# Spreading a weight split over the last projections, on a kernel of infini-attention and a Fourier layer

## The chip, the core and the metric

The kernel runs on one core of a Trainium2 chip. The metric is the device time of one execution in microseconds (us), lower is better. The core has TensorE for matrix products, VectorE and ScalarE for elementwise work, GpSimd for elementwise work in on-chip memory, and SyncE, which here only issues DMAs. In the profile they are called PE, DVE, ACT, POOL and SP. Every engine works through its own instructions strictly in the order of the program and waits where an operand is not there yet.

## What is computed

Two branches work on 2048 tokens of width 576, and their outputs stand side by side.

```python
# branch A: 32 heads of width 18, 4 segments of 512 tokens, a memory M, z carried from segment to segment
for s in range(4):
    logits = q[s] @ k[s].T * scale + mask          # mask: -1e9 where query index < key index
    a_dot  = softmax(logits) @ v[s]
    a_mem  = (phi(q[s]) @ M) / (phi(q[s]) @ z + 1e-6)
    out[s] = g * a_mem + (1 - g) * a_dot
    M, z   = M + phi(k[s]).T @ v[s], z + sum(phi(k[s]))
A = concat(out) @ wo
# branch B: Fourier mixing, real part of a transform along features and then along tokens
a, b = x @ dft_hid_re.T, x @ dft_hid_im.T
B = dft_seq_re @ a - dft_seq_im @ b
```

All of it is wanted at about fp32 accuracy, so the kernel splits each operand into a rounded part and the rest ("hi" and "lo") and multiplies three times, or writes it as three bf16 parts.

## The kernel before, in words

The order of every engine's instructions is written out by hand. The program has a first phase (lines 147 to 552) that runs over the four segments `s`, and a second phase that interleaves the attention of branch A with the Fourier products of branch B on TensorE until the end.

In the first phase each segment has nine projections of queries and keys (`project_qk`, 14 matmuls each; `m` is the tile: 0 to 3 are queries, 4 to 7 keys, 8 holds what is left of both) and then four rounds `j` of the value projection (`project_v`). A round has two halves `h` of 14 matmuls and, from the second segment on, the two parts of the lookup in the memory (`lookup`), which stand after the halves on TensorE. I number a round's four TensorE steps: half 0, look part 1, half 1, look part 2. In the last segment (`s == 3`) the projections come in the order m = 0, 1, 2, 3, 8, 4, 5, 6, 7, so that `n`, the place in that order, is 4 for m = 8 and 5 to 8 for m = 4 to 7.

All these products are written to one ring of five PSUM buffers with the tag `acc`. A product can start only when the product five places earlier has been read out. After tile 8 the ring goes on as m = 4, 5, 6, 7, then round 0: half 0 (in the buffer of m = 8), look part 1 (of m = 4), half 1 (of m = 5), look part 2 (of m = 6), then round 1: half 0 (of m = 7), look part 1 (of round 0's half 0), and so on.

A projected key tile of the last segment is read out as three bf16 parts: `p0` by ScalarE (L272), the rest `r` by VectorE (L273), and then, in the nested function `rest`, `p1` from `r` (L282 on GpSimd or L284 on ScalarE) and `p2` by GpSimd (L285). `rest` is called one `tick()` later, just after `project_qk` has returned. The last reader of the PSUM buffer is `r`. A half of the value projection is read by ScalarE (L321) and VectorE (`vr`, L324); VectorE's instructions of a lookup end with `w` (L412), which is the last reader of look part 2.

The first phase also prepares the second one. `h_load` fetches the five row blocks `k` of the Fourier weights along the features, `h_split(0, k)` splits a block with `split_wk`: ScalarE rounds it (L130, twice for k = 4) and VectorE subtracts (L124; for k = 4 L126 and L127). `c_cut(n, dve)` splits input chunk `n` of the Fourier branch: ScalarE rounds two pieces (L448, L450), and one tick later VectorE subtracts twice (L453, L455). The change calls the Fourier weights "memory weights".

In the second phase the first TensorE work is one score product (L735) and `hidden(0, 0)`, which multiplies chunk 0 with the split weights in two halves (L619 to L624). The second of these halves is written to a PSUM bank that the first phase's last look part 2 had, so it starts when the last `w` is done.

Of the kernel before, what the change touches and what calls it, by code (L numbers as in the profile page):

```python
# [40 lines left out]
def infini_attention_and_fnet(ctx: ExitStack, tc: tile.TileContext, xT, wqk, w8, wv, wo, beta, xtT, cT, hT, out):  # L41
    nc = tc.nc
    act, dve, pool, pe = nc.scalar, nc.vector, nc.gpsimd, nc.tensor
# [38 lines left out]
    def chain(o, terms):  # L82
        for n, (a, b) in enumerate(terms):
            pe.matmul(o, a, b, start=n == 0, stop=n == len(terms) - 1)  # L84
# [3 lines left out]
    def later(n, fn, *a):  # L88
        due.setdefault(clock[0] + n, []).append((fn, a))

    def tick():
        clock[0] += 1
        for fn, a in due.pop(clock[0], ()):
            fn(*a)
# [26 lines left out]
    def split_wk(w, k, raw, wait=0):  # L121
        def low():
            if k < 4:
                dve.tensor_tensor(w[1][k], raw, w[0][k].bitcast(F32), OP.subtract)  # L124
            else:
                dve.tensor_tensor(w[2][:64], raw[:64], w[2][:64].bitcast(F32), OP.subtract)  # L126
                dve.tensor_tensor(w[3][64:], raw[64:], w[3][64:].bitcast(F32), OP.subtract)  # L127

        for t in (w[0][k],) if k < 4 else (w[2], w[3]):
            act.activation(t, raw, AF.Copy)  # L130
        if wait:
            later(wait, low)
        else:
            low()
# [6 lines left out]
    def weight(mk):  # L141
        return [[mk() for _ in range(4)] for _ in range(2)] + [mk() for _ in range(2)]

    def wide_tile(cols):
        return lambda: wide.tile([P, cols], F32R, name="wide", tag="wide")
# [68 lines left out]
    def phi(e, sources, hi, lo):  # L214
        for to, src in sources:
            act.activation(to, src, AF.Relu, scale=-1.0)
        act.activation(e, e, AF.Exp, scale=-1.0)
        for to, src in sources:
            dve.scalar_tensor_tensor(to, src, 0.0, to, op0=OP.max, op1=OP.add)
        dve.tensor_copy(hi, e)  # L220
        pool.tensor_tensor(lo, e, hi.bitcast(F32), OP.subtract)

    def qk_terms(s, m):
        xh, xl, xt = X[s]
        W, c = (WQ, m) if m < 4 else (WK, m - 4) if m < 8 else (W8, 0)
        cs = slice(c * P, (c + 1) * P)
        terms = []
        for k in range(4):
            terms += [(W[0][k][:, cs], xh[k]), (W[0][k][:, cs], xl[k]), (W[1][k][:, cs], xh[k])]
        return terms + [(W[2][:, cs], xt), (W[3][:, cs], xt)]  # L230
# [3 lines left out]
    def warm_up():  # L234
        o = ps.tile([P, L], F32, name="warm", tag="acc", bufs=5)
        for _ in range(38):
            pe.matmul(o[:, :P], ones, ones, start=True, stop=True)

    def open_qk(s):
        for m in range(4):  # L240
            FIRST[m] = ps.tile([P, L], F32, name="qk", tag="acc", bufs=5)
        terms = [qk_terms(s, m) for m in range(4)]
        edges = (0, 6, 14) if s else (0, 1, 2, 3, 6, 9, 14)
        for a, b in zip(edges, edges[1:]):
            for m in range(4):
                for n in range(a, b):
                    pe.matmul(FIRST[m], *terms[m][n], start=n == 0, stop=n == 13)  # L247
                if s and m == 0 and a:
                    accumulate(3, (1,))
            if s and a == 0:  # L250
                accumulate(3, (0,))
# [8 lines left out]
    def project_qk(s, m):  # L260
        if m in FIRST:
            o = FIRST.pop(m)
        else:
            o = ps.tile([P, L], F32, name="qk", tag="acc", bufs=5)
            chain(o, qk_terms(s, m))
        if m >= 4 and s < 3:
            KF[m] = sk.tile([P, L], F32, name="kf", bufs=5)
            act.activation(KF[m], o, AF.Copy)
        p = sb.tile([P, 3, L], BF16, name="p", tag="p", bufs=5)
        r = sb.tile([P, L], F32, name="r", tag="r", bufs=3)  # L270
        p0, p1, p2 = (p[:, 2 - i] if 4 <= m < 8 else p[:, i] for i in range(3))
        act.activation(p0, o, AF.Copy)  # L272
        dve.tensor_tensor(r, o, p0, OP.subtract)  # L273
        if s and (m < 4 or m == 8):
            n = P if m < 4 else 64
            c = m if m < 4 else 4
            e = sb.tile([P, L], F32, name="qe", bufs=2)[:n]
            phi(e, ((e, o[:n]),), pq_hi[:n, c], pq_lo[:, c] if m < 4 else pq_hi[64:, c])

        def rest():  # L280
            if m in (5, 6, 7):
                pool.tensor_copy(p1, r)  # L282
            else:
                act.activation(p1, r, AF.Copy)  # L284
            pool.tensor_tensor(p2, r, p1, OP.subtract)  # L285
            if m < 8:
                later(1, dma, (qd if m < 4 else kd)[s][(m % 4) * P:(m % 4 + 1) * P, :3], p)
            else:
                later(1, dma, qd[s][4 * P:, :3], p[:64])
                for i in range(3):  # L290
                    later(1, dma, kd[s][4 * P:, 2 - i], p[64:, i])

        later(1, rest)

    def k_natural(j):
# [124 lines left out]
    def h_load(ri, k):  # L420
        HRAW[ri, k] = sb.tile([P, D], F32, name="raw", tag="raw", bufs=5 if ri == 0 else 3)
        dma(HRAW[ri, k], hT[ri, k])

    def h_split(ri, k):
        if k == 0:
            HW[ri] = weight(wide_tile(D))
        split_wk(HW[ri], k, HRAW.pop((ri, k)), 2 * ri)
# [13 lines left out]
    def c_cut(n, engine=pool):  # L441
        if n < len(CHUNKS):
            raw = c_raw.pop(n)
            hi = sr.tile([P, 4, P], F32R, name="chi", bufs=3)
            lo = sr.tile([P, 4, P], F32R, name="clo", bufs=3)
            t = sr.tile([P, P], F32R, name="xtail", bufs=3) if CHUNKS[n][2] == 5 else None
            c_split[n] = hi, lo, t
            act.activation(hi, raw[:, :4], AF.Copy)  # L448
            if t is not None:
                act.activation(t, raw[:, 4], AF.Copy)  # L450

            def low():
                engine.tensor_tensor(lo, raw[:, :4], hi.bitcast(F32), OP.subtract)  # L453
                if t is not None:
                    engine.tensor_tensor(t[64:], raw[64:, 4], t[64:].bitcast(F32), OP.subtract)  # L455
            later(1, low)
# [40 lines left out]
    for s in range(NSEG):  # L497
        more = s < 3
        if s == 0:
            warm_up()  # L500
        open_qk(s)
        if s:
            memory()
        else:
            tick()
        for n, m in enumerate((0, 1, 2, 3, 8, 4, 5, 6, 7) if s else range(9)):
            project_qk(s, m)
            tick()
            if not more and n in (5, 7):
                h_split(0, (n - 5) // 2)  # L510
            if s and n < (8 if more else 4):
                copy_parts(s - 1, 2 * n)
                copy_parts(s - 1, 2 * n + 1)
            if s in (1, 2) and n >= 4:
                load_x(s + 1, n - 4)
            if not more and n == 0:
                for k in range(5):
                    h_load(0, k)
            if not more and n == 4:
                p1k.close()  # L520
                sr = ctx.enter_context(tc.tile_pool(name="sb2r", bufs=1, side="right", reuse_waits="tile"))
                attention_tiles()
            if not more and n == 4:
                c_load(0)
                c_load(1)
                stacks(sr, 0)
                stack_load(0)
            if not more and n == 6:
                c_load(2)
        for j in range(4):  # L530
            project_v(s, j, lookup(s, j) if s else iter(()))
            tick()
            for k in ((0, 1), (2, 3), (4,), ())[j] if s == 0 else ():
                load_x(1, k)
            if more and j in (1, 2):
                split_x(s + 1, j - 1)
            if not more and j == 1:
                stacks(sr, 1)
            if not more and j == 2:
                attention_constants()  # L540
            if not more and j == 0:
                h_split(0, 2)
                h_split(0, 3)
            if not more and j == 1:
                h_split(0, 4)
                c_cut(0, dve)
                c_cut(1, dve)
            if not more and j in (1, 3):
                c_load(3 + j // 2)
            if more and j:  # L550
                accumulate(j - 1)
# [512 lines left out]
```

## Time and profile before

| what | value |
| --- | --- |
| time, median of 3 runs | 1001.66 us (1001.62 to 1001.66) |
| the profiled execution: its time, its span | 1000.29 us, 998.5 us |
| TensorE clock granted | 1.000 |
| PE busy | 988.2 us, 99% |
| DVE busy | 754.1 us, 76% |
| ACT busy | 710.6 us, 71% |
| POOL busy | 635.8 us, 64% |
| last segment's projections, value rounds, first Fourier product | from about 178 us to 228 us of the span |

The busy shares are averages over the whole span. A row of the timeline has the start and the length of an instruction in us, its engine, line and operation, the tiles written and read, their shape, and in brackets how long the engine had been idle before and what released it. A count such as x2 puts neighbouring equal instructions together.

### The profile page before, as it was taken

Reading aid. Unit: us, or ns where it says so; the run is one execution under the profiler, and the core shown is the slowest. Engines: PE = TensorE matmul, PEld = TensorE weight load, DVE = VectorE, ACT = ScalarE, POOL = GpSimd, SP = SyncE. Lnnn points to the kernel's source line nnn. Section 1 sums busy time; section 2 is a strip of 40 time slices with the busy share of each in tenths; the row PEclk is TensorE's granted clock in tenths of the full one; section 3 lists DMA queues with packets and bytes.
Section 4 is the critical chain, followed back from the end, with each engine's and each line's share of the span. In section 5 each row is a group of like instructions: output and inputs, shape, how many; then the busy total and the mean of one; then the engine's idle time right before and its main releaser. Section 6 shows DMA issues by size and latency. Waiting matters only on the chain.

```text
span 998.5 us, 25584 instructions
## 1 busy us (share of the span) xinstructions
PE 988.2 (99%) x9294; PEld 923.3 (92%) x9294; DVE 754.1 (76%) x2049; ACT 710.6 (71%) x1677; POOL 635.8 (64%) x700
## 2 busy tenths in 40 slices
PE   9999999989999999999999999999999999999998
PEld 7989989889999999999999999999999999999998
DVE  6657668594678777878898888898888899998321
ACT  6667576653887877878788788877767777777243
POOL 2657576676767667666866777776767767767000
PEclk9999999999999999999999999999999999999999
DMA  7447456767578899899999997779998999988555
GB/s 253 170 126 245 187 177 239 239 231 227 147 178 212 217 236 231 201 243 221 249 231 232 211 221 198 180 200 226 222 234 215 239 238 243 244 187 188 139 153 137
DMA packets 305182, 208.92 MB, mean 209 GB/s; under 512 B 206240, under 2 KB 259872, under 8 KB 305056
## 3 DMA queue, kind: packets, MB, share of 16 engines
q1 hardware_dynamic: 304816, 207.15, 79.7%
q8 instruction: 73, 1.20, 0.5%
q14 instruction: 53, 0.43, 0.1%
q10 hardware_dynamic: 240, 0.14, 0.1%
HBM read 121.32 MB, written 57.93 MB: 180 GB/s over the span
## 4 chain that ended last, share of the span: by engine, by line
PE 89%; DVE 5%; ACT 3%; issue 1%; DMA 1%; POOL 1%; SPq 0%; DVEq 0%; ACTq 0%; POOLq 0%
PE d L574 39%; PE s L735 7%; PE d L84 6%; PE pv L853 4%; PE v L84 4%; PE qk L247 4%; PE d L619 3%; PE d L620 3%; PE d L621 3%; PE qk L84 3%; PE pv L854 2%; PE m L360 1%; PE t L809 1%; PE t L812 1%; DVE plo L836 1%
## 5 line engine op out<-in xcount | busy, mean ns | idle before, releaser
L741 DVE CUSTOM_DVE_ANT_0 s<-s,causal 128x128 f32<-128x128 f32 (+3 forms) x512 | 249.9, 498 | 101.5 <-PE s L735 92.4
L453 POOL TENSOR_TENSOR clo<-craw,chi 128x512 fp32r<-128x512 f32 x158 | 216.4, 1370 | 96.7 <-ACT chi L448 65.3
L574 PE MATMUL d<-wide,chi 128*128 128x288 f32 x1408 | 266.2, 306 | 0.4 <-DVE y L644 0.4
L574 PEld LDWEIGHTS d<-wide,chi 128*128 128x128 f32 x1408 | 211.8, 189 | 2.4 <-DVE y L644 0.6
L574 PE MATMUL d<-wide,clo 128*128 128x288 f32 x704 | 177.5, 319 | 0.0
L775 POOL TENSOR_TENSOR hl<-pf,hl 128x768 f16<-128x768 f32 x64 | 112.9, 1763 | 70.0 <-ACT hl L771 54.2
L821 ACT ACTIVATE phi<-t 128x384 f16<-128x384 f32 x128 | 61.7, 482 | 103.6 <-PE t L818 103.5
L735 PE MATMUL s<-ks,qs 108*128 108x128 bf16 (+3 forms) x512 | 133.7, 304 | 0.5 <-DVE negm L741 0.4
L764 ACT ACTIVATE pf<-s,nb 128x128 f32<-128x128 f32 (+3 forms) x256 | 128.1, 526 | 6.2
L836 DVE TENSOR_TENSOR plo<-pf,phi 128x384 f16<-128x384 f32 (+1 forms) x128 | 126.2, 986 | 0.0
L574 PE MATMUL d<-ab,chi 128*128 128x288 f32 x640 | 126.0, 306 | 0.0
L574 PEld LDWEIGHTS d<-wide,clo 128*128 128x128 f32 x704 | 118.6, 189 | 1.6
L822 ACT ACTIVATE pf<-t 128x384 f32<-128x384 f32 (+1 forms) x192 | 99.6, 519 | 6.2 <-PE t L809 6.0
L448 ACT ACTIVATE chi<-craw 128x512 fp32r<-128x512 f32 x160 | 100.2, 627 | 2.3 <-PE d L574 1.2
L574 PEld LDWEIGHTS d<-ab,chi 128*128 128x128 f32 x640 | 98.5, 189 | 0.6
L771 ACT ACTIVATE hl<-pf 128x768 f16<-128x768 f32 (+1 forms) x128 | 87.4, 730 | 2.0
L619 PE MATMUL d<-wide,chi 128*128 128x288 f32 x256 | 84.1, 329 | 2.8 <-ACT xtail L450 2.8
L574 PE MATMUL d<-ab,clo 128*128 128x288 f32 x320 | 84.8, 314 | 0.0
L620 PE MATMUL d<-wide,chi 128*128 128x288 f32 x256 | 75.6, 295 | 0.0
L621 PE MATMUL d<-wide,clo 128*128 128x288 f32 x256 | 75.5, 295 | 0.0
L775 DVE TENSOR_TENSOR hl<-pf,hl 128x512 f16<-128x512 f32 x64 | 67.5, 1055 | 0.1
L836 POOL TENSOR_TENSOR plo<-pf,phi 128x384 f16<-128x384 f32 x64 | 59.3, 927 | 13.0 <-ACT pf L822 10.4
(204 smaller groups left out, 2497.2 us busy)
## 6 DMA issues: line engine op xcount, KB each, us to landing
craw<-cT SPq DMA_DIRECT2D x128, 256.0 KB
ks<-kd SPq DMA_DIRECT2D x32, 432.0 KB
qs<-qd SPq DMA_DIRECT2D x32, 432.0 KB
craw<-xtT SPq DMA_DIRECT2D x32, 320.0 KB
vd<-vs SPq DMA_DIRECT2D x16, 440.0 KB
vst<-vd SPq DMA_DIRECT2D x32, 220.0 KB
qd<-p SPq DMA_DIRECT2D x16, 384.0 KB
kd<-p SPq DMA_DIRECT2D x16, 384.0 KB
```

Of the source, the lines that this page charges most:

```text
L84: pe.matmul(o, a, b, start=n == 0, stop=n == len(terms) - 1)
L448: act.activation(hi, raw[:, :4], AF.Copy)
L453: engine.tensor_tensor(lo, raw[:, :4], hi.bitcast(F32), OP.subtract)
L574: pe.matmul(o[h], a, b[:, h * 288:h * 288 + 288], start=start, stop=stop)
L619: pe.matmul(o, xh[:, k], wl[k][:, cs], start=k == 0, stop=False)
L620: pe.matmul(o, xh[:, k], wh[k][:, cs], start=False, stop=False)
L621: pe.matmul(o, xl[:, k], wh[k][:, cs], start=False, stop=False)
L735: pe.matmul(o[:, c:c + w], q[:, i * P:w], k[:, :w], start=True, stop=True)
L741: dve.tensor_tensor_reduce(o[:, c:c + w], o[:, c:c + w], CAUSAL[0][:, L - w:], scale=scale, scalar=-LOWEST, op0=OP.add, op1=OP.min, accum_ ...
L764: act.activation(f[:, FIRST_COL[i]:FIRST_COL[i] + w], o[:, c:c + w], AF.Exp, bias=nb[:, i:i + 1], scale=-1.0)
L775: engine.tensor_tensor(hl[:, 1, a:b], f[:, a:b], hl[:, 0, a:b], OP.subtract)
L836: (pool if kind == 2 else dve).tensor_tensor(lo[:, a:b], f[:, a:b], hi[:, a:b], OP.subtract)
```

## The change

In the last segment alone, three things move.

1. `p1` of the key tiles 5, 6 and 7 is made by ScalarE (L284) and no longer by GpSimd (L282).
2. The five `h_split(0, k)` follow the five projections n = 4 to 8, one after each. Before, k = 0 and 1 followed n = 5 and 7, k = 2 and 3 came after value round 0, and k = 4 after round 1.
3. `c_cut(0)` comes after round 0 and `c_cut(1)` after round 1. Before, both came after round 1. VectorE's part is issued one round later in both cases.

No instruction is added or taken away apart from the engine of three `p1`.

```diff
         def rest():
-            if m in (5, 6, 7):
+            if m in (5, 6, 7) and s < 3:
                 pool.tensor_copy(p1, r)
             else:
                 act.activation(p1, r, AF.Copy)
...
             project_qk(s, m)
             tick()
-            if not more and n in (5, 7):
-                h_split(0, (n - 5) // 2)
+            if not more and n >= 4:
+                h_split(0, n - 4)
...
-            if not more and j == 0:
-                h_split(0, 2)
-                h_split(0, 3)
-            if not more and j == 1:
-                h_split(0, 4)
-                c_cut(0, dve)
-                c_cut(1, dve)
+            if not more and j < 2:
+                c_cut(j, dve)
```

## The prediction

> **What bounds the kernel now.** I read the page first, then the waits of TensorE over the whole span, then busy times by stretch around the change, then the timelines of the engines there.
>
> ```profile
> PE 988.2 (99%) x9294; PEld 923.3 (92%) x9294; DVE 754.1 (76%) x2049; ACT 710.6 (71%) x1677; POOL 635.8 (64%) x700
> ...
> PE 89%; DVE 5%; ACT 3%; issue 1%; DMA 1%; POOL 1%; SPq 0%; DVEq 0%; ACTq 0%; POOLq 0%
> ```
>
> The first row is busy time, the second the chain that ended last. TensorE is busy 99% of the span, so whatever doesn't reach TensorE costs and brings nothing. The waits of TensorE say where it stood still:
>
> ```profile
> PE d L619 <- ACT xtail L450: 2.8, 1, 2.8
> PE warm L237 <- DVE ones L68: 1.1, 1, 1.1
> ```
>
> One wait after the start is above a microsecond, 2.8 us once, at L619. The change sits just ahead of it. By stretch (columns: PE, PEld, DVE, ACT, POOL busy, granted clock, DMA share and rate):
>
> ```profile
> 199.10:219.60 20.50, 20.50 (x163) 20.46 (x161) 18.50 (x38) 13.42 (x34) 17.97 (x16) 1.00 0.71 247
> 219.60:224.50 4.90, 2.09 (x15) 1.86 (x15) 4.65 (x13) 2.15 (x7) 2.29 (x6) 1.00 0.38 152
> 224.50:260.00 35.50, 35.50 (x268) 33.99 (x269) 18.48 (x61) 18.03 (x47) 22.88 (x27) 1.00 0.55 172
> ```
>
> In the four value rounds (first row) TensorE is full and VectorE nearly so, 18.5 of 20.5 us. Then VectorE works off what it has left while TensorE waits (second row), and from 224.5 on TensorE has no gap (third row). So a move of TensorE's start at 224.50 moves the end by as much, up or down. On TensorE's timeline:
>
> ```profile
> 204.11 0.47 PE L84 MATMUL v<-wide,xh 128*128 128x288 f32 x2
> ...
> 206.00 0.34 PE L393 MATMUL look<-md,pq_hi 128*128 128x152 f32 x2
> ...
> 219.44 0.39 PE L735 MATMUL s<-ks,qs 108*128 108x512 bf16 x1
> ...
> 221.40 0.29 PE L624 MATMUL d<-wide,xtail 128*128 128x288 f32 x1
> 224.50 0.37 PE L619 MATMUL d<-wide,chi 128*128 128x288 f32 x1 [2.81 <-ACT xtail L450]
> ```
>
> These are round 1's half 0 (204.11), round 1's look part 1 (206.00), the first score product (219.44), the end of the first half of the Fourier product (221.69) and its second half. That half waits for a PSUM bank, whose last reader is `w` (L412) of round 3; the view names a ScalarE instruction that ended at about the same time. VectorE at its end:
>
> ```profile
> 217.84 0.68 DVE L453 TENSOR_TENSOR clo<-craw,chi 128x512 fp32r<-128x512 f32 x1
> 218.56 1.15 DVE L455 TENSOR_TENSOR xtail<-craw,xtail 64x128 fp32r<-64x128 f32 x1
> 219.74 1.64 DVE L453 TENSOR_TENSOR clo<-craw,chi 128x512 fp32r<-128x512 f32 x1
> 221.39 0.42 DVE L455 TENSOR_TENSOR xtail<-craw,xtail 64x128 fp32r<-64x128 f32 x1
> 221.84 0.82 DVE L324 TENSOR_TENSOR vr<-v,vs 128x288 f32<-128x288 f32 x2
> ...
> 224.16 0.19 DVE L412 TENSOR_TENSOR w<-look,g 128x32 f32<-128x32 f32 x1
> ```
>
> `w` ends at 224.35 and TensorE goes on 0.15 later. Before it VectorE has 4.0 us of chunk splits, while round 3's values are there already.
>
> **What the change takes away at that end.** The splits of k = 2, 3 and 4 and one of the two chunks leave VectorE's queue in the value rounds. How early could round 3 then be read out? ScalarE's copy of its half 1:
>
> ```profile
> 219.31 0.42 ACT L321 ACTIVATE vs<-v 128x288 bf16<-128x288 f32 x1 [1.35 <-PE v L84]
> ```
>
> It waited for TensorE and ends at 219.73, 0.29 after the score product starts. From the second `vr` to the end of `w` VectorE needs 224.35 - 221.84 - 0.41 (the first `vr`, half of 0.82) = 2.1 us. So `w` could end 0.33 + 2.1 = 2.47 after the score product starts, and TensorE go on 2.62 after it; now it is 224.50 - 219.44 = 5.06. That is a gain of 2.44 us, if nothing else moves. The remaining wait would be about 0.4 us (the first half ends 2.25 after the score product).
>
> **What it puts in front of the value rounds.** ScalarE and VectorE over tiles 8, 4, 5, 6 now, with GpSimd:
>
> ```profile
> 196.66 0.57 ACT L272 ACTIVATE p<-qk 128x512 bf16<-128x512 f32 x1
> 198.11 0.63 ACT L284 ACTIVATE p<-r 128x512 bf16<-128x512 f32 x1 [0.87 <-DVE r L273]
> 198.64 0.67 ACT L130 ACTIVATE wide<-raw 128x576 fp32r<-128x576 f32 x1
> ```
>
> ```profile
> 197.40 0.68 DVE L273 TENSOR_TENSOR r<-qk,p 128x512 f32<-128x512 f32 x1
> 199.35 1.46 DVE L124 TENSOR_TENSOR wide<-raw,wide 128x576 fp32r<-128x576 f32 x1 [1.27 <-ACT wide L130]
> 200.73 1.28 DVE L273 TENSOR_TENSOR r<-qk,p 128x512 f32<-128x512 f32 x2
> 201.92 1.13 DVE L124 TENSOR_TENSOR wide<-raw,wide 128x576 fp32r<-128x576 f32 x1
> 202.98 0.68 DVE L273 TENSOR_TENSOR r<-qk,p 128x512 f32<-128x512 f32 x1
> 204.80 0.82 DVE L324 TENSOR_TENSOR vr<-v,vs 128x288 f32<-128x288 f32 x2 [1.15 <-POOL p L285]
> ```
>
> ```profile
> 197.64 1.29 POOL L221 TENSOR_TENSOR pq_hi<-qe,pq_hi 64x512 fp32r<-64x512 f32 x1 [2.33 <-DVE pq_hi L220]
> 199.02 1.17 POOL L285 TENSOR_TENSOR p<-r,p 128x512 bf16<-128x512 f32 x1
> ```
>
> Now ScalarE makes `p0` of tiles 5, 6 and 7 without looking back, because GpSimd makes their `p1`; VectorE gets tile 5's and 6's `r` in one go (x2). The `r` of tile 7 ends at 203.66, and TensorE wants its buffer at 204.11 (round 1's half 0). That is 0.45 us of room, and `vr` of round 0 ends its first half at 205.2 for TensorE's 206.00.
>
> After the change ScalarE's queue per key tile reads `p0`, `p1`, round of k, then the next tile's `p0`; VectorE's reads split of k, `r`, split of k+1, `r`. ScalarE's `p1` waits for `r`, the split waits for ScalarE's round, which stands behind `p1`, and the next `r` stands behind the split. The two engines take turns. Behind the waiting `p1` on ScalarE stand the next round and the next `p0`; behind VectorE's waiting split stands the `r` that frees TensorE's buffer.
>
> How long is a turn? A split alone takes about 0.70 (0.68 in the row of L453 at 217.84, of nearly the same size). The L124 at 199.35 took 1.46: GpSimd's L285 ran until 200.19, and the split ended 0.62 after that. The slow L453 and L455 above are of the same kind. So a VectorE subtraction with both inputs in on-chip memory waits until a running GpSimd subtraction ends, and then needs 0.62. In the changed order GpSimd's `p2` starts about 0.13 after `p1` ends, 0.4 us before the split is ready. So a turn is: `p1` 0.63, start of `p2` 0.13, `p2` 1.17, split 0.62, `r` 0.66 = 3.2 us. Without GpSimd in the way it would be `p1` 0.53 to the next start, round 0.67, split 0.70, `r` 0.68 = 2.6 us. I take 3.2, since both L124 rows above that overlap a GpSimd subtraction show the wait.
>
> The Trainium skill, page "SBUF — State Buffer", section "Who interferes with whom", says that a VectorE instruction with two SBUF inputs and a GpSimd one that reads SBUF exclude each other for the whole instruction, and that the one that was issued first wins. By that rule the turn is 3.2 us wherever `p2` starts ahead of the split and 2.6 where it starts behind; the rows here agree with the first half, and none shows the second with these tiles.
>
> The schedule that follows: VectorE is free at 197.40, where `r` of tile 4 starts now. The split of k = 0 goes first (0.70) and `r` of tile 4 ends at 198.8. Three turns of 3.2 for tiles 5, 6, 7 end at 208.4, against 203.66 now; GpSimd still has tile 8's work (the L221 and L285 rows) in the first turn, which makes it 0.1 to 0.2 shorter: 208.2. Then `p1`, `p2` (to 210.1), the two subtractions of k = 4 (0.62 and 0.70, 211.5) and the first `vr` of round 0 (0.41, 211.9). Its PSUM buffer is round 1's look part 1: TensorE gets there at 212.0 and not at 206.00. On the way it waits in three places: round 0's look part 2 behind `r` of tile 6 (205.1 where TensorE is there 0.3 ahead of 204.11: 1.3 us), round 1's half 0 behind `r` of tile 7 (208.3 + 0.1 for 204.11 + 1.3: 3.0 us), look part 1 behind `vr` (212.0 for 208.4 + 1.9: 1.7 us). In all 6.0 us are lost. In TensorE's order this is one delay, and the later rounds run at their own pace behind it, because VectorE has no weights left to split there: per round two `vr` and a lookup, 2.5 us, and in two of them a chunk of at most 2.1, against 5 us of TensorE.
>
> The sum: 6.0 lost ahead of round 1, 2.44 gained at the end, 3.6 us net. TensorE's start at 224.50 becomes about 228.1. The profiled execution (1000.29) would become 1003.9, and the median 1001.66 becomes **1005.3 us**; the profiled one lay 1.4 below the median, and I add the difference to the median.
>
> ```profile
> 175.97 2.79 SPq L422 DMA_DIRECT2D raw<-hT x5
> ```
>
> ```profile
> 202.38 1.14 POOL L282 CAST p<-r 128x512 bf16<-128x512 f32 x1
> ```
>
> What I cost at nothing: the loads of the weights, issued by 178.8 (SyncE's row), 18 us ahead of the first round of them; the three `p1` off GpSimd (this one 1.14, held up by the split at 201.92), since TensorE waits for GpSimd nowhere in these stretches; SyncE's writes of keys and values, which move with the tiles and are read when the attention reaches the fourth segment. If the weights had not landed at 196.7, each microsecond would be one more on the path.
>
> **Bounds.** If GpSimd never stands in the way, turns of 2.6 end tile 7 at 206.6, and round, split, split and `vr` follow at 209.6: 3.75 lost, 1.3 net, 1003.0. If each of the later splits costs 1.5, as L124 at 199.35 did, a turn is 3.4 and the tail 0.8 longer: 1.4 more than the forecast, 1006.7.
>
> **Rivals.** First, *GpSimd is out of the way*: 1003.0, as just worked out; for it speaks only that GpSimd loses the three `p1` and may take `p2` at another moment. Second, *faster*: TensorE isn't caught, because the `r` of tile 7 still ends before 204.1 and the first `vr` before 206.0; then the 2.44 us come in full, 999.2 us. That decides by whether the turns overlap: from 198.8 that leaves 5.3 us for three turns, 1.8 a turn, and `p1`, split and `r` alone are 0.63 + 0.70 + 0.68 = 2.0. I see no way but a wrong reading of the buffer ring. Third, *the clock drops*: the wait ahead of round 1's half 0 is some 3.0 us long, and two others stand around it with little work between. The 2.81 us gap at 224.50 left the granted clock at 1.00 (third row by stretch). If it fell to half for as long as the wait, 3 us of matmuls would take twice as long, up to 3 more: 1007 to 1008.3. The Trainium skill, page "TensorE: Matmul & The Clock Gate", Part 1, puts the drop after an idle window of about 3.4 us; by that rule the one wait is just short of it.
>
> **Chances and range.** Forecast 0.76, GpSimd out of the way 0.10, faster 0.08, clock 0.06. The range takes in the first two and the upper bound: 1002.8 to 1007.0. The measurement tells 0.2%, 2.0 us, from no change, so slower begins at 1003.7. Faster 0.08; the same 0.10; slower 0.82.
>
> **What would show it.** In the changed profile: TensorE's waits have three new entries of about 1.3, 3.0 and 1.7 us, behind L273 twice and L324, between 203 and 213 us; L619's wait is below 0.8 us; the `r` of tiles 4 to 7 stand 3.2 us apart; L284 on ScalarE waits for L273 four times; the second Fourier half starts near 228. Wrong would be: `r` of tile 7 before 204.1, no new wait, or a new wait beyond 228.

## The result, and the profile after

The changed kernel takes 1005.13 us (median of 14 runs, 1003.58 to 1009.05), the kernel before, run beside it, 1001.97 us (median of 14, 999.99 to 1004.21). The ratio is 1.0033, with a 95% interval of 1.0022 to 1.0043: 3.2 us slower by the medians, where 3.6 were forecast. The profiled execution of the changed kernel is the longest of its runs, 1009.05 us with a span of 1007.3, and that matters below.

The page of the changed kernel, the busy times and the chain that ended last:

```profile
PE 994.2 (99%) x9294; PEld 928.1 (92%) x9294; DVE 752.6 (75%) x2049; ACT 713.2 (71%) x1680; POOL 632.3 (63%) x697
...
PE 87%; DVE 5%; ACT 4%; DMA 2%; issue 1%; POOL 1%; SPq 0%; DVEq 0%; POOLq 0%; ACTq 0%
```

TensorE has the same 9294 matmuls and is busy 6.0 us longer. The same matmuls took longer in places, which is a matter of its clock. The waits of TensorE over the whole span:

```profile
PE v L84 <- DVE r L273: 2.5, 1, 2.5
PE qk L247 <- ACT wide L130: 1.8, 1, 1.8
PE look L399 <- DVE r L273: 1.3, 1, 1.3
PE warm L237 <- DVE ones L68: 1.1, 1, 1.1
PE s L730 <- DVE negm L736: 0.4, 2, 0.2
PE d L614 <- DVE w L412: 0.4, 1, 0.4
```

The 2.8 us ahead of the second Fourier half have become 0.4 (last row; five lines have gone from the file ahead of it, so L619 is L614 here). In their place stand two waits for `r` of key tiles. The 1.8 us at L247 lie in the first 10 us of the kernel, which the change doesn't touch. The profile before has a wait of 0.6 us there. Behind the longer one the clock of this execution was at half for 3.4 us (the granted clock, the column ahead of the last two, is 0.83, 0.50 and 0.82 from 10 to 12, 12 to 14 and 14 to 16 us):

```profile
0.00:20.00 20.00, 17.04 (x87) 13.91 (x88) 11.47 (x20) 11.21 (x19) 2.08 (x16) 0.91 0.81 258
```

VectorE's timeline over the key tiles and into round 0:

```profile
200.71 0.68 DVE L273 TENSOR_TENSOR r<-qk,p 128x512 f32<-128x512 f32 x1
202.66 1.15 DVE L124 TENSOR_TENSOR wide<-raw,wide 128x576 fp32r<-128x576 f32 x1 [1.27 <-ACT wide L130]
203.73 0.68 DVE L273 TENSOR_TENSOR r<-qk,p 128x512 f32<-128x512 f32 x1
205.68 1.51 DVE L124 TENSOR_TENSOR wide<-raw,wide 128x576 fp32r<-128x576 f32 x1 [1.27 <-ACT wide L130]
207.11 0.68 DVE L273 TENSOR_TENSOR r<-qk,p 128x512 f32<-128x512 f32 x1
209.06 1.24 DVE L124 TENSOR_TENSOR wide<-raw,wide 128x576 fp32r<-128x576 f32 x1 [1.27 <-ACT wide L130]
210.22 0.68 DVE L273 TENSOR_TENSOR r<-qk,p 128x512 f32<-128x512 f32 x1
212.17 1.25 DVE L126 TENSOR_TENSOR wide<-raw,wide 64x576 fp32r<-64x576 f32 x1 [1.27 <-ACT wide L130]
213.45 0.76 DVE L127 TENSOR_TENSOR wide<-raw,wide 64x576 fp32r<-64x576 f32 x1
214.24 0.82 DVE L324 TENSOR_TENSOR vr<-v,vs 128x288 f32<-128x288 f32 x2
```

In every turn VectorE is idle for 1.27 us until ScalarE has rounded the next block. ScalarE in turn, waits from 199 to 216 us (total, times, longest):

```profile
ACT p L284 <- DVE r L273: 5.4, 4, 1.7
```

It waits four times for `r`. Two engines that are busy 71 and 75% of the span hold each other up, and the `r` of tiles 4 to 7 stand 3.0, 3.4 and 3.1 us apart. TensorE behind them:

```profile
207.84 0.41 PE L399 MATMUL look<-md,pq_hi 128*128 128x304 f32 x1 [1.25 <-DVE r L273]
...
210.96 0.85 PE L84 MATMUL v<-wide,xh 128*128 128x288 f32 x2 [2.52 <-DVE r L273]
...
214.75 0.71 PE L393 MATMUL look<-md,pq_hi 128*128 128x152 f32 x2
...
219.91 0.30 PE L399 MATMUL look<-md,pq_hi 128*128 128x304 f32 x1
...
230.39 0.39 PE L730 MATMUL s<-ks,qs 108*128 108x512 bf16 x1
...
233.03 0.37 PE L614 MATMUL d<-wide,chi 128*128 128x288 f32 x1 [0.39 <-DVE w L412]
```

Everything in this execution stands 2.64 us later than before when it reaches the last segment: the first L219 of tile 8 starts at 198.98 and not at 196.34. Taken off, round 1's look part 1 starts at 212.11 instead of 206.00, 6.1 us late, and the second Fourier half at 230.39 instead of 224.50, 5.9 us late. At 210.96 two matmuls that took 0.47 us take 0.85. By stretch, with the clock in the same column:

```profile
208.40:211.00 2.60, 0.08 (x2) 0.05 (x1) 1.84 (x2) 1.18 (x4) 1.16 (x1) 0.67 0.89 259
211.00:214.75 3.75, 3.68 (x14) 3.33 (x15) 2.52 (x4) 3.00 (x8) 1.17 (x1) 0.50 1.02 396
214.75:219.60 4.85, 4.85 (x21) 4.85 (x22) 2.29 (x9) 2.23 (x5) 2.38 (x2) 0.51 0.35 138
219.60:233.00 13.40, 13.04 (x102) 12.78 (x101) 10.51 (x31) 7.10 (x20) 7.36 (x9) 1.00 0.46 172
```

TensorE's clock fell to half in the second wait and came back at about 219.5. While TensorE would have waited for `vr` anyway (until 214.65) the slow clock costs nothing; from there look part 1 and half 1 of round 1 took 219.91 - 214.75 = 5.2 us, where the kernel before needs 208.87 - 206.00 = 2.9: 2.3 us lost. The row of the kernel before that this rests on:

```profile
208.87 0.30 PE L399 MATMUL look<-md,pq_hi 128*128 128x304 f32 x1
```

So the excess in this execution is 2.6 us from the start of the kernel (the longer wait there and the slow clock behind it), 6.1 from the waits ahead of round 1's look part 1, 2.3 from the clock, less 2.4 at the second Fourier half: 8.6 of the 8.8 us between the spans.

### The profile page after: what moved, and what is told of

It is laid out like the page before. It is cut to its first block, busy times and chain, and to the rows that moved or that the text cites. A ratio compares the mean times of both kernels' runs of the same rounds, so it can differ in the third digit from the quotient of the medians.

```text
span 1007.3 us, 25584 instructions
## 1 busy us (share of the span) xinstructions
PE 994.2 (99%) x9294; PEld 928.1 (92%) x9294; DVE 752.6 (75%) x2049; ACT 713.2 (71%) x1680; POOL 632.3 (63%) x697
## 4 chain that ended last, share of the span: by engine, by line
PE 87%; DVE 5%; ACT 4%; DMA 2%; issue 1%; POOL 1%; SPq 0%; DVEq 0%; POOLq 0%; ACTq 0%
PE d L569 38%; PE s L730 7%; PE d L84 6%; PE v L84 5%; PE pv L848 4%; PE qk L247 3%; PE d L614 3%; PE d L615 3%; PE d L616 3%; PE pv L849 2%; PE qk L84 2%; PE m L360 1%; PE t L804 1%; PE look L393 1%; DVE r L273 1%
## 5 line engine op out<-in xcount | busy, mean ns | idle before, releaser
L614 PE MATMUL d<-wide,chi 128*128 128x288 f32 x256 | 84.1, 329 | 0.4 <-DVE w L412 0.4
```

The source lines that it names most:

```text
L614: pe.matmul(o, xh[:, k], wl[k][:, cs], start=k == 0, stop=False)
```

## The experiments

My theory: ScalarE's `p1` and the splits together make the two engines take turns; GpSimd's `p2` makes each turn longer; the clock drop comes on top. Rivals: one part of the change does it alone; the clock drop is the cost, or none of it.

**The changed kernel again, and with work in its waits.** No edit for the first; the second adds matmuls whose results nobody reads:

```diff
+    def fill(n):
+        for _ in range(n):
+            pe.matmul(m_ps[0][:, 0], pq_hi[:, 0, :P], md[:, 0, 0], start=True, stop=True, skip_group_check=True)
...
+            if s == 3 and (j, h) == (1, 0):
+                fill(20)                       # ahead of round 1's half 0
...
+            if s == 3 and (j, h) in ((0, 1), (1, 0)):
+                fill(9 if h else 12)           # ahead of the look parts
             next(meanwhile, None)
```

> The changed kernel once more, beside the others of this call. If the added time is the waits of TensorE alone, all its runs lie about 3.6 us above those of the kernel before. If the clock drops after those waits in some executions, its runs spread over several us, and the granted clock that each run lists falls as the time rises: half clock for 1 us of work lowers the mean over 1000 us by 0.0005 and costs up to 0.5 us.

> The changed kernel with 9, 20 and 12 extra matmuls (128x152, results not used) on TensorE at the three places where it waits in value rounds 0 and 1, about 0.11 us each, so 1.0, 2.2 and 1.3 us of work inside waits of 1.3, 2.5 to 3.0 and 1.7 us. They wait for nothing and delay nothing. If the clock drop behind the waits costs time, the clock stays at 1.00 through the value rounds, look part 1 of round 1 stays where it is (6.1 us late), and the time is about 2 us below the changed kernel's profiled execution: 3.6 us above the kernel before, with little spread. If the drop costs nothing or comes from something else, the time and its spread are those of the changed kernel.

Measured beside the kernel before at 1001.78 us: the changed kernel 1005.83 (1003.97 to 1007.31; ratio 1.0036, 1.0023 to 1.0048), with the filler 1004.60 (1003.99 to 1005.23; 1.0027, 1.0018 to 1.0036). The clock listed by the six runs of the first goes from 0.994 in two of the three longest to 0.998 in the shortest; in the ten runs of the second it is 0.999 or 1.000. TensorE with the filler, and two stretches of it:

```profile
204.33 1.12 PE L308 MATMUL m<-md,pq_hi 128*128 128x152 f32 x9
205.74 0.41 PE L407 MATMUL look<-md,pq_hi 128*128 128x304 f32 x1 [0.29 <-DVE r L273]
206.17 2.40 PE L308 MATMUL m<-md,pq_hi 128*128 128x152 f32 x20
208.87 0.54 PE L84 MATMUL v<-wide,xh 128*128 128x288 f32 x2 [0.30 <-DVE r L273]
...
212.67 0.45 PE L401 MATMUL look<-md,pq_hi 128*128 128x152 f32 x2 [0.38 <-DVE vr L330]
```

```profile
204.00:208.00 4.00, 3.71 (x33) 3.56 (x32) 2.73 (x3) 1.71 (x4) 1.64 (x2) 1.00 0.69 191
208.00:212.00 4.00, 3.70 (x31) 3.55 (x30) 2.69 (x4) 3.06 (x8) 1.17 (x1) 1.00 0.99 358
```

The clock stays at 1.00. Look part 1 stands at 212.67, which is 212.14 on the scale of the kernel before (its L219 of tile 8 is 0.53 later), 6.1 us late as in the changed kernel, and the second Fourier half at 228.77 - 0.53 = 228.24, 3.7 us late. So the turns cost 3.7 us net without any clock drop, and with the drop the two profiles of the changed kernel have 5.9 and 6.0. By the medians of these 6 and 10 runs the drop costs 1.2 us, and 0.5 against the 14 runs above (1005.13); its size in the median isn't settled, and not all executions pay the 2.2. The filled kernel is 2.8 us above the kernel before where I had expected 3.6; most runs of the kernel before lose some clock too, as shown below. The second profile of the changed kernel, its slow stretch:

```profile
206.00:217.00 11.00, 9.07 (x38) 8.73 (x39) 6.62 (x14) 5.72 (x14) 4.14 (x4) 0.53 0.66 240
```

**One part at a time.** `p1` alone on the kernel before; splits and cuts alone (the changed kernel with `p1` back on GpSimd); cuts alone on the kernel before:

```diff
# p1 alone, against the kernel before
-            if m in (5, 6, 7):
+            if m in (5, 6, 7) and s < 3:
# splits and cuts alone, against the changed kernel
-            if m in (5, 6, 7) and s < 3:
+            if m in (5, 6, 7):
# cuts alone, against the kernel before
-                c_cut(0, dve)
-                c_cut(1, dve)
+            if not more and j < 2:
+                c_cut(j, dve)
```

> The kernel before with p1 of key tiles 5, 6 and 7 on ScalarE, splits and chunk cuts as before. Theory of the turns (ScalarE's p1 waits for VectorE's r, and VectorE's split for ScalarE behind it): p1 alone makes half of the turns, r of tile 7 ends near 206.4 instead of 203.7, TensorE loses about 2.4 us ahead of round 1 and keeps its wait at the second Fourier half (VectorE still has weights and both chunks in the rounds): 2.5 to 3 us slower. Rival, the splits alone do it: no change (within 0.5 us).

> The changed kernel with p1 of tiles 5, 6 and 7 back on GpSimd, splits and chunk cuts moved. Theory of the turns: ScalarE runs ahead, VectorE works without gaps, r of tile 7 ends near 205.1 and the first vr near 207.8, TensorE loses about 2 us, gains 2.4 at the second Fourier half: within 0.7 us of the kernel before. Rival, the splits alone do it: 3.6 us slower, like the changed kernel. If p1 on GpSimd meets the splits at the shared port more often than the schedule has it, in between.

> The kernel before with the chunk cuts alone moved (one after each of value rounds 0 and 1). VectorE has the same work in the value rounds, so it ends at the same time: no change within 0.5 us. TensorE's wait of 2.8 us may move from the second Fourier half to earlier places. Rival, the gain at the end comes from the cuts and not from the splits: up to 2 us faster.

| kernel | median, us | the kernel before beside it | ratio, 95% interval |
| --- | --- | --- | --- |
| the change | 1005.83 | 1001.78 | 1.0036, 1.0023 to 1.0048 |
| `p1` alone | 1003.45 | 1001.78 | 1.0013, 1.0005 to 1.0022 |
| splits and cuts alone | 1000.24 | 1001.78 | 0.9982, 0.9973 to 0.9991 |
| cuts alone | 1000.19 | 1001.39 | 0.9991, 0.9982 to 1.0000 |

TensorE's waits in the profiles of these three, in this order (the rows behind the start of the kernel that are above 0.45 us, and L614):

```profile
PE v L84 <- DVE r L273: 2.2, 1, 2.2
PE d L619 <- ACT xtail L450: 1.7, 1, 1.7
```

```profile
PE v L84 <- DVE r L273: 0.7, 1, 0.7
PE look L393 <- DVE vr L324: 0.5, 1, 0.5
...
PE d L614 <- DVE w L412: 0.4, 1, 0.4
```

```profile
PE look L393 <- DVE vr L324: 1.5, 1, 1.5
...
PE d L619 <- DVE w L412: 0.9, 1, 0.9
```

With `p1` alone a wait for `r` of 2.2 us appears, and 1.7 us stay at the second Fourier half: slower, as the theory had it, by 1.7 us in the medians for the 2.5 to 3 expected, and by 227.92 - 0.56 - 224.50 = 2.9 between the profiles (0.56 is the shift of its L219 of tile 8). The theory had the 2.8 us at the second Fourier half stay whole. They are 1.7 here because the clock was at half from 207.1 to 210.5: half 0 of round 1 took 210.57 - 207.07 = 3.5 us and not 1.9, and that ate part of the wait. VectorE, which sets the start of the second Fourier half, stood idle 0.5 us more for it, so about that much of the 2.9 is the clock.

With the splits and cuts alone the waits are 0.7, 0.5 and 0.4 where `p1` on top makes them 1.3, 2.5 and the slow clock; look part 1 of round 1 is 208.49 - 0.55 - 206.00 = 1.9 us late, as the theory had it, where the change makes it 6.1. So neither part makes the 3 to 4 us alone; both do it together. Moving `p1` back is worth 5.6 us by the medians (1005.83 to 1000.24), and 4.2 between two profiles at full clock (228.24 with the filler, 224.04 without the moved `p1`).

The splits and cuts came out 1.5 us faster, and I had expected no change within 0.7. The cuts alone came out 1.2 us faster, with an interval that reaches 1.0000, and I had expected no change within 0.5; their total of waits is still 2.4 us, but in two pieces. In their profiles the second Fourier half is only 0.5 (224.59 - 0.55 = 224.04) and 0.1 us (223.91 + 0.49 = 224.40) earlier than in the profile of the kernel before, as the schedule says. Most of the rest fits the clock of the kernel before. Of its 25 runs beside the cuts alone five list 1.000 (999.63 to 1001.06, median 1000.71) and 19 list 0.997 or 0.998 (1000.77 to 1003.58), while the splits and cuts alone list 0.999 or 1.000 in all 11 runs and the cuts alone 0.999 or 1.000 in eight of 11. The profiled execution of the kernel before was one at 1.000; most of its executions are not. No profile shows where they lose it; that it is at the wait of 2.8 us is argued from the versions that don't have that wait.

**GpSimd out of the way.** The changed kernel with the third part of the key tiles 4 to 7 of the last segment left out:

```diff
-            pool.tensor_tensor(p2, r, p1, OP.subtract)
+            if s == 3 and 4 <= m < 8:
+                pool.memset(p2, 0.0)
+            else:
+                pool.tensor_tensor(p2, r, p1, OP.subtract)
```

> The changed kernel with the third part (p2) of the last segment's key tiles 4 to 7 left out: GpSimd fills it with zeros, which reads nothing. If GpSimd's subtraction is what makes a turn 3.2 us, turns become 2.6: r of tile 7 ends some 1.3 us earlier, TensorE reaches round 1's look part 1 about 4.1 us late instead of 6.1, and the kernel is 1.3 to 1.9 us slower than the one before. If a turn's length comes from ScalarE and VectorE alone, the turns stay at 3.2 and the time at that of the changed kernel.

Measured: 1002.92 us beside 1001.39 (ratio 1.0019, 1.0009 to 1.0029), 1.5 us slower than before and inside the 1.3 to 1.9 expected. VectorE in two of its turns, GpSimd's zero fills, and the stretch from 204 to 212 us:

```profile
200.89 0.68 DVE L273 TENSOR_TENSOR r<-qk,p 128x512 f32<-128x512 f32 x1
202.84 0.76 DVE L124 TENSOR_TENSOR wide<-raw,wide 128x576 fp32r<-128x576 f32 x1 [1.27 <-ACT wide L130]
203.52 0.68 DVE L273 TENSOR_TENSOR r<-qk,p 128x512 f32<-128x512 f32 x1
205.47 0.76 DVE L124 TENSOR_TENSOR wide<-raw,wide 128x576 fp32r<-128x576 f32 x1 [1.27 <-ACT wide L130]
206.15 0.68 DVE L273 TENSOR_TENSOR r<-qk,p 128x512 f32<-128x512 f32 x1
...
201.42 1.92 POOL L286 MEMSET p<- 128x512 bf16 x4
...
204.00:212.00 8.00, 5.70 (x25) 5.55 (x26) 5.23 (x13) 6.22 (x15) 0.00 (x0) 0.62 0.91 298
```

These turns are 2.63 us and L124 takes 0.76 instead of 1.15 to 1.51. That is the 2.6 of the lower bound. (The first turn, where GpSimd still subtracts for tile 8, takes 3.0.) GpSimd's zero fill, which reads nothing, doesn't hold the split up: the one at 202.84 starts beside it and takes 0.76, as the one at 205.47 does with GpSimd idle. The Trainium skill, page "SBUF — State Buffer", section "Who interferes with whom", says just this: a VectorE instruction with two SBUF inputs contends with a GpSimd one that reads SBUF and not with one that only writes it.

The turns are shown by these rows; that the time came out inside the range is partly luck. The `r` of tile 7 ends 1.3 us earlier than in the changed kernel, as expected, but look part 1 is 4.6 us late and not 4.1 (210.41 + 0.19 for 206.00; its L219 of tile 8 is 0.19 earlier), and the second Fourier half 3.5 (227.78 + 0.19 for 224.50). The clock stood at half for 6.8 us in this profile, eight of the nine runs list 0.998 or less, and most runs of the kernel before pay for their clock too.

**A version that beats both.** The splits go where the two engines wait for each other anyway, in the last segment's tiles 1, 2, 3 and 8, ahead of the exponential; `p1` stays on GpSimd:

```diff
+        if s == 3 and m in (1, 2, 3, 8):
+            h_split(0, (1, 2, 3, 8).index(m))
         if s and (m < 4 or m == 8):
...
-            if not more and n in (5, 7):
-                h_split(0, (n - 5) // 2)
+            if not more and n == 5:            # first version
+                h_split(0, 4)
...
-            if not more and j == 0:
-                h_split(0, 2)
-                h_split(0, 3)
-            if not more and j == 1:
-                h_split(0, 4)
-                c_cut(0, dve)
-                c_cut(1, dve)
+            if not more and j == 0:            # second version, instead of the one above
+                h_split(0, 4)
+            if not more and j < 2:             # both
+                c_cut(j, dve)
```

> A version of my own: the kernel before with the splits of k = 0 to 3 put into the last segment's tiles m = 1, 2, 3 and 8, after r and ahead of phi, where ScalarE waits 0.9 us for r and VectorE 1.4 us for the exponential in every tile; the split of k = 4 after tile 4; p1 on GpSimd as before; chunk cuts moved as in the change. By the theory of the turns no r gets later and VectorE enters the value rounds with less: nothing lost ahead of round 1, 2.4 us gained at the second Fourier half, so about 2 us below the version with the splits alone, 998.3 to 999.5. Rival: the splits push the exponentials of tiles 1 to 8 back by 0.7 to 1.3 each and TensorE waits for their buffers: no better than the splits alone.

> The version with the splits in the query tiles, with the split of k = 4 after value round 0 instead of after tile 4. There VectorE's two subtractions stand between tile 4's r and those of tiles 5 to 7, and TensorE waits 1.0 us for tile 5's r in round 0. In round 1 VectorE needs 2.5 us of TensorE's 5, so there is room for 1.5 to 2.4. By the theory the 1.0 us goes and nothing takes its place: about 998 us, some 3.5 us below the kernel before. Rival: k = 4 meets GpSimd's long subtractions in round 1 and is waited for there: no change against the version before it.

The first takes 998.86 us beside 1001.39 (0.9973, 0.9964 to 0.9982), the second 998.40 beside 1001.50 (0.9964, 0.9950 to 0.9978). The first is inside the 998.3 to 999.5 expected, though one `r` did get later and TensorE waited for it. The waits above 0.45 us behind the start, of the first:

```profile
PE v L84 <- DVE r L273: 1.0, 1, 1.0
PE trm L789 <- POOL mb L785: 0.8, 1, 0.8
```

In the second no wait above 0.4 us is left behind the start; the two that went stood at the fifth split and at the start of the attention. It is 3.1 us faster than the kernel before by the medians, where the change is 3 to 4 slower. Between two profiled executions at full clock the gain is 998.5 - 996.7 = 1.8 us; part of the rest fits the clock that most executions of the kernel before lose. Its gain over the first was expected at 1.0 us and is 0.5 by medians of 11 and 5 runs, which doesn't separate the two.

## Why the prediction was right, and where not

- **What bounds the kernel**: right. From the second Fourier half to the end the profile after needs 774.3 us, the profile before 774.0. A move of that start moves the end.
- **The gain at the end**: right. TensorE goes on 233.03 - 230.39 = 2.64 us after the score product where 2.62 was worked out and 5.06 stood before, with 0.39 us of wait left. (The working has 0.33 + 2.1 = 2.47, where its rows give 0.29 + 2.1 = 2.39; by them it would be 2.54.)
- **The turns**: right. 3.0, 3.4 and 3.1 us for 3.2; the `r` of tile 7 ends at 210.90 - 2.64 = 208.3 for 208.2, the first `vr` at 214.65 - 2.64 = 212.0 for 211.9, look part 1 is 6.1 us late for 6.0. GpSimd's share is shown by leaving `p2` out: turns of 2.63, and `r` of tile 7 at 207.0.
- **Three waits of 1.3, 3.0 and 1.7 us**: two came, 1.25 and 2.52. The third was filled by slow matmuls; with the filler it is back as 1.46 of filler and 0.38 of wait.
- **The rival of the clock**: mis-sized. I gave it 0.06, because a wait of 2.81 us in the one profile before had left the clock at 1.00. That was one execution. The runs' clocks show that most executions of the kernel before lose some clock, and all 20 of the changed one list 0.998 or less; both of its profiles have the drop. I took the slow stretch to be as long as the wait, 3 us, and priced it at up to 3. It lasted 10.2 us in both profiles; about half of that lay where TensorE would have waited in any case, and 2.3 us were lost, 0.5 to 1.2 by the medians. So the second Fourier half stood at 230.4 and 230.5 in these profiles (on the scale of the kernel before) and not near 228 as forecast; with the filler it stands at 228.2.
- **The sum**: 3.6 us forecast, 3.2 and 4.1 measured in two sets of runs. The 3.7 that the turns cost without a drop are shown. That the medians come out near it is partly two clock terms that cancel: the changed kernel's own drop, 0.5 to 1.2 us, and the one that the kernel before pays and that goes with its wait, about 0.7 (1000.71 at full clock for 1001.39 of all).
- **That the difference of the profiled execution to the median carries over**: wrong as a step. The profile before was 1.4 us below the median, because it was an execution at full clock, the profile after 3.9 above.

## What to carry to other kernels

When work is moved between engines, write down for each queue what stands directly behind the instruction that waits, and follow the circle: two engines with a quarter of their time free can still pass one token back and forth, and the reader that frees the accumulator pays. Put early work where an engine already waits for another, not where it still runs ahead; here the same splits, so placed and without the moved `p1`, made the kernel 3 us faster and not 3 slower. One wait of about 2 us on TensorE costs more than its length in some executions, so look at the clock of all runs before a profile is taken for typical. Two short waits well apart (1.5 and 0.9 us with 5.5 us of work between them, in the version with the cuts alone) left the clock at 0.999 or 1.000 in eight of 11 runs, where one of 2.8 us left it there in six of 25.

## What the runs showed of the hardware that I had not expected

TensorE's clock fell to half although no wait was longer than 2.52 us: in the first profile after, 0.67 as the mean from 208.40 to 211.00 puts the fall near 209.3, 0.8 us into the second wait and 2.7 after the start of the first (206.59). It stayed at half until about 219.5, some 10.2 us, with 8.5 us of nearly unbroken matmuls in it. In the second profile after it was at half from 206.5 to 216.8, again 10.2 us. In the profile of `p1` alone it fell near 207.1, at the end of a single wait of 2.24 us, and was back near 210.5, after 3.4 us (0.89 as the mean of 204 to 208, 0.87 of 210 to 212). In the profile without `p2` it was at half from 206.0 to 212.8, 6.8 us, and in the first profile after also from 11.3 to 14.7, 3.4 us, behind the wait of 1.82 us at L247.

So the five slow stretches lasted one, two or three times 3.4 us. In the 3.4 us that end at each fall TensorE had stood idle for 1.6 to 2.4 us in all (1.75 at the start of the kernel and 2.1 in the first profile after, 2.4 in the second, 2.2 with `p1` alone, 1.6 without `p2`). A wait of 2.81 us left the clock at 1.00 in the profile before, so the length of a wait alone doesn't decide it; what does is not shown here.

The Trainium skill, page "TensorE: Matmul & The Clock Gate", Part 1, has the clock halve after an idle window of about 3.4 us and return after about as long of busy time, by a window that runs freely. The multiples of 3.4 and the spread between runs fit such a window; the falls without a wait of that length and the returns after 6.8 and 10.2 us do not follow from what it states.
